# Attention and two MLPs on one core: code products put in front of a value burst, a scaling put one slot later, VectorE's work dealt out anew, and a rearranged start

## The chip, the cores and the metric

One core of a Trainium2 chip runs the whole program in one launch. The time is the device time of that launch in microseconds (us). Before the change three runs took 793.62, 793.74 and 791.83 us, median 793.62. TensorE (PE) does the matrix products, VectorE (DVE), ScalarE (ACT) and GpSimd (POOL) the elementwise work, and DMA queues, issued mostly by SyncE (SP), move data. PSUM has eight banks, in which matrix products land.

## The reference

The attention has 16 heads (batch 2 by 8), 768 rows, 64 columns. Each row of q and of k gets a 6-bit code, and a score counts only where the codes agree:

```python
q_bits = (np.einsum('bhsd,dk->bhsk', q, proj) > 0)
k_bits = (np.einsum('bhsd,dk->bhsk', k, proj) > 0)
mask = q_bucket[:, :, :, None] == k_bucket[:, :, None, :]
scores = np.where(mask, scale * np.matmul(q, k.transpose(0, 1, 3, 2)), -1000000000.0)
attn = np.exp(scores - np.max(scores, axis=-1, keepdims=True))
attn = attn / (np.sum(attn, axis=-1, keepdims=True) + 1e-09)
out = np.matmul(attn, v)
```

Its 1536 by 512 output goes through two MLPs (512 to 2048 to 512). The first has g = h * tanh(log(1 + exp(h))), the second a rational function of h. All is float32.

## The kernel before

**Heads and slots.** The attention is laid out in slots, six to a head, one for each block of 128 keys (`c`). In a slot TensorE computes the scores of one block, `sp` (function `st`, L380: four products, a large part `qB` and a small part `qX`, with K and the codes in one stacked operand `kk`), and ACT takes their exponential `e` (L385). Beside that stands `mp` (function `smax`, L347: two products) of a head or two later, of which DVE takes the row maximum `m` (L351). When a head's six maxima are there, `fin_a` and `fin_b` (L357, L360, L366) put them by four small DMAs, two from SP's queue and two from POOL's, into a row of `qB`, so that the scores come out with the maximum taken off.

**Bursts.** After some slots TensorE runs products of other shapes in a row: `pv` (function `pv`, L287: exponentials times V, for two blocks at a time, in slots 3, 5 and 7 of the head, thus slots 3, 5 and the next head's 1), `dn` (function `dsum`, L406: sums of the exponentials, four products at once in four column groups of 32), `vsp` (function `vsum`, L274: sums of V, in even heads, for the pair of heads), and `cp` (function `codes`, L287: the projections whose signs are the codes). The signs of `cp` are taken by DVE for k (`code_k`, L324, into `kk`) and by ACT for q (`code_q`, L333, into `qB`); both read the one PSUM tile `cp`.

**Division.** `devac` copies `dn` out (L431), `gather` brings it into 24 rows by DMA, `recip` is a chain of five short operations on DVE (L452 to L458), `store` and `spread` send the result through memory to all partitions, and `norm` (L482), `xhi` and `xlo` scale and split the head pair's output for the first MLP.

**What sets the order.** The order is written out, not scheduled. A table, `order`, gives for each function the slot in which it runs, counted from the first slot of its head; -16 is sixteen slots ahead. Within a slot the functions run in the order of the table, and each engine runs its instructions in the order in which they were written. The list `start` writes out the first head's chain by hand (`warm` are small products that keep TensorE busy, `khi`, `hi` and `lo` split q and k into a large and a small part). `tail(i)` runs what is left of the attention within the iterations of the first MLP.

**Buffers.** `sp`, `mp` and `vsp` take turns in three buffers of two PSUM banks (pool `ps`). Which one a tile takes follows from the order in which they are freed in the program. `dn` and `cp` share one bank, `pv` has another.

**DVE's other work.** The weights of the first MLP come as 64-bit numbers; DVE turns them into float32 with three operations a part (L100, L103, L106), in slots of the attention and beyond.

Of the kernel before, what the change touches and what calls it, by code (L numbers as in the profile page):

```python
# [44 lines left out]
def attention_moe_moe(ctx: ExitStack, tc: tile.TileContext, kq, v, proj2, cst, eye, w1, w2, ab, out):  # L45
# [11 lines left out]
    def f32(ap):  # L57
        return ap.bitcast(F32)
# [111 lines left out]
    def attention(actx, tctx):  # L170
# [26 lines left out]
        def memsets():  # L197
            nc.vector.memset(ones, 1.0)
            nc.vector.memset(wones, 1.0)
            nc.gpsimd.memset(cs_t, 0.0)  # L200
            nc.gpsimd.memset(cs_t[:, 1:2], -1.0)
            nc.gpsimd.memset(cs_t[:, 2:3], 1.0)
            for i in range(4):
                nc.gpsimd.memset(f32(KK[i])[32:64, 0], 0.0)
            for i in range(2):
                nc.gpsimd.memset(f32(SM[i]), 0.0)
            nc.gpsimd.memset(bias[:, 1:2], 1.000001)
# [25 lines left out]
                fn = fn or lo_of("lo", h)  # L233
                fn(qX[h % 4], raws[h], qB[h % 4])

        def khi(h, i):
            nc.scalar.activation(out=KK[h % 4][64:128, i], in_=raws[h][0:64], func=ACT.Copy)

        def move_k(h):
            if 0 <= h < B * H:  # L240
# [39 lines left out]

# [13 lines left out]

        ct = {}


        def codes(h):
            if not 0 <= h < B * H:
                return  # L300
            ct[h] = [pvp.tile([128, 512], F32, tag="dn", name="cp")] * 2
            if h == 0:
                ct[h][1] = pvp.tile([128, 512], F32, tag="pv", name="wm")
            for t in ct[h][0:1 + (h == 0)]:
                both(t, p_raw, raws[h], start=True, stop=True)


        warm_up = []

        def warm(n):  # L310
            if 0 in ct:
                t = ct[0][1]
            else:
                if not warm_up:
                    warm_up.append(ps.tile([128, 2, 512], F32, tag="s", name="wm"))
                t = warm_up[0][:, 0]
            for _ in range(n):
                nc.tensor.matmul(out=t[0:32, HALF:512], lhsT=ones, rhs=wones, start=True, stop=True)

        def code_k(h):  # L320
            if not 0 <= h < B * H:
                return
            for a in range(2):
                nc.vector.tensor_scalar(  # L324
                    out=qhalf(KK[h % 4][0:32, 0], a), in0=ct[h][0][64 * a:64 * a + 32, 0:HALF],
                    scalar1=cs_t[:, 1:2], scalar2=cs_t[:, 2:3], op0=ALU.is_gt, op1=ALU.mult,
                )

        def code_q(h):
            if not 0 <= h < B * H:  # L330
                return
            for a in range(2):
                nc.scalar.activation(  # L333
                    out=qhalf(qB[h % 4], a)[0:32], in_=ct[h][1][64 * a + 32:64 * a + 64, 0:HALF],
                    func=ACT.Sign, bias=cs_t[:, 0:1],
                )

        mt = {}

# [87 lines left out]
        def devac(h):  # L427
            if not 0 <= h < B * H:
                return
            dv = cs_p.tile([128, HALF], F32, tag="dv", name="dv")  # L430
            nc.scalar.activation(out=dv, in_=pvt.pop((h, "d"))[:, 0:HALF], func=ACT.Copy)  # L431
            Rt[h] = dv

        def gather(h):
            if not 0 <= h < B * H:
                return
            dv = Rt.pop(h)
            cs = cs_p.tile([24, 2, 32], F32, tag="cs", name="cs")
            for n in range(2):
                nc.sync.dma_start(  # L440
                    out=cs[:, n], in_=dv[64 * n:64 * n + 64:32].rearrange("t (a i) -> t a i", i=32)
                )
            Rt[h] = cs

        def recip(h):
            if not 0 <= h < B * H:
                return
            cs = Rt.pop(h)
            rc = cs_p.tile([24, 32], F32, tag="rc", name="rc")

            z = cs_p.tile([24, 32], F32, tag="z", name="z")
            nc.vector.tensor_tensor(out=rc, in0=cs[:, 0], in1=cs[:, 1], op=ALU.add)  # L452
            nc.vector.tensor_scalar(
                out=z, in0=rc, scalar1=0.0, scalar2=float(np.float32(1e-9)) / (S * TINY) - 1.0, op0=ALU.is_equal, op1=ALU.mult
            )
            nc.vector.tensor_scalar(out=rc, in0=rc, scalar1=1e-9, scalar2=None, op0=ALU.add)
# [67 lines left out]
        def first(f, n):  # L524
# [48 lines left out]
        for name, fn, at, per in order:  # L573
# [29 lines left out]
        start = (  # L603
            ("load", 0), ("get", 0), ("get", 1), ("load", 1), ("load", 2), ("warm", 5), ("hi", 0), ("codes", 0),
            ("khi", 0, 0), ("lo", 0), ("code_q", 0), ("code_k", 0), ("warm", 1), ("hi", 1), ("lo", 1), ("khi", 0, 1),
            ("get", 2), ("move_x", 0), ("smax", 0, 0), ("warm", 2), ("move_h", 0), ("hi", 2), ("lo", 2), ("smax", 0, 1),
            ("move_k", 1), ("warm", 2), ("smax", 0, 2), ("load", 3), ("warm", 2), ("smax", 0, 3), ("codes", 1),
            ("smax", 0, 4), ("warm", 2), ("code_q", 1), ("smax", 0, 5), ("fin_a", 0), ("fin_b", 0), ("code_k", 1),
            ("warm", 6), ("move_k", 2), ("load_v", 0), ("move_x", 1), ("smax", 1, 0), ("smax", 1, 1), ("move_h", 1),
            ("coef",),  # L610
        )

        def run():
            memsets()
            fns = {o[0]: o[1] for o in order}
            fns.update(get=get, coef=coef, khi=khi)
            for name, *k in start:
                if name == "warm":
                    warm(*k)
                    continue  # L620
                done.add(("move_k" if name == "khi" else name, tuple(k[:1]) if name == "khi" else tuple(k)))
# [10 lines left out]
    def moe(mctx, tctx, tail):  # L632
# [114 lines left out]
        def run():  # L747
# [70 lines left out]
            for i in range(-5, len(seq) + 5):  # L818
# [102 lines left out]
```

## Time and profile before

| | us |
|---|---|
| median of three runs | 793.62 (791.83 to 793.74) |
| the profiled execution | 791.69 |
| its span | 789.8 |
| TensorE, busy | 774.2 (98%) |
| VectorE, busy | 593.7 (75%) |
| ScalarE, busy | 422.5 (53%) |
| first scores (`sp` of head 0) | at 19.67 |
| first scores of head 1 | at 36.57 |
| first product of the MLPs | at 259.65 |

The span begins and ends with the first and last record; the profiled execution's own time is 1.89 us longer. A row of the timeline gives the start, the duration (of merged records, from the first start to the last end), engine, line and operation, output <- inputs, shape and the count of records; a matrix product of float32 leaves two records. Matrix products are pipelined, so that their durations overlap, and the difference between two starts tells what one costs. In brackets stands the idle time before an instruction and what ended it.

### The profile page before, as it was taken

The numbers are of one execution on the slowest core, as the hardware profiler recorded it, in microseconds if no ns is written. First come the engines' busy times: TensorE is split into PE (matmuls) and PEld (weight loads), VectorE is DVE, ScalarE is ACT, GpSimd is POOL, SyncE is SP. The second block draws the span as 40 slices with busy tenths as digits, with TensorE's granted clock in tenths as the row PEclk, the third lists the DMA queues.
The fourth block names the chain that finished last, engine by engine and source line by source line (L and its number), as shares of the span: only waits on it lengthen the run. The fifth ranks groups of instructions, "written<-read, shape, count | busy, mean of one in ns | idle before, by whom it ended". The sixth has DMA issues, their size and how long they took to land.

```text
span 789.8 us, 10934 instructions
## 1 busy us (share of the span) xinstructions
PE 774.2 (98%) x3788; PEld 572.4 (72%) x3788; DVE 593.7 (75%) x1100; ACT 422.5 (53%) x684; POOL 71.6 (9%) x100
## 2 busy tenths in 40 slices
PE   7899999999999999999999999999999999999998
PEld 4556555555555778888888888887888888888886
DVE  5587778778772599846556677659998888888886
ACT  3455565655555443331212334368886867777664
POOL 4223214124121000000000000000000000000000
PEclk9999999999999999999999999999999999999999
DMA  4847666554651444424555587620000100000001
GB/s 124 211 128 202 174 162 175 141 142 121 174 166 31 127 137 148 131 87 145 171 157 149 165 255 256 202 80 1 0 1 1 53 1 1 1 36 18 1 0 54
DMA packets 57031, 85.50 MB, mean 108 GB/s; under 512 B 20496, under 2 KB 28688, under 8 KB 56976
## 3 DMA queue, kind: packets, MB, share of 16 engines
q1 hardware_dynamic: 55952, 84.77, 36.4%
q8 instruction: 30, 0.49, 0.3%
q14 instruction: 25, 0.20, 0.1%
q0 software_dynamic: 1024, 0.03, 0.1%
HBM read 57.71 MB, written 14.73 MB: 92 GB/s over the span
## 4 chain that ended last, share of the span: by engine, by line
PE 88%; DVE 6%; DMA 2%; ACT 1%; issue 1%; SPq 1%; POOL 0%; DVEq 0%; ACTq 0%
PE h L665 29%; PE y L685 16%; PE y L683 15%; PE sp L380 9%; PE pv L287 8%; PE mp L347 5%; PE dn L406 4%; PE cp L287 2%; DVE w L70 1%; DVE m L351 1%; DMA kk<-qB 1%; DVE t L103 1%; DMA vf<-v 1%; DVE r L106 1%; DVE gl L70 1%
## 5 line engine op out<-in xcount | busy, mean ns | idle before, releaser
L665 PE MATMUL h<-xh,w 128*128 128x512 f32 x768 | 205.0, 389 | 0.0
L665 PEld LDWEIGHTS h<-xh,w 128*128 128x128 f32 x768 | 144.1, 188 | 30.6 <-issue 0.6
L351 DVE TENSOR_REDUCE m<-mp 128x1 f32<-128x768 f32 x96 | 91.3, 955 | 50.2 <-PE mp L347 49.0
L385 ACT ACTIVATE e<-sp 128x768 f32<-128x768 f32 x96 | 77.1, 810 | 80.8 <-PE sp L380 79.4
L70 DVE TENSOR_TENSOR gl<-ep,gh 128x512 fp32r<-128x512 f32 x96 | 65.9, 687 | 69.4 <-ACT ep L709 68.6
L708 ACT ACTIVATE gh<-h 128x512 fp32r<-128x512 f32 x48 | 28.7, 598 | 154.7 <-PE h L665 141.5
L665 PE MATMUL h<-xl,w 128*128 128x512 f32 x384 | 102.7, 389 | 0.0
L685 PE MATMUL y<-w,gh 128*128 128x512 f32 x384 | 96.3, 389 | 0.0
L683 PE MATMUL y<-gh,w 128*128 128x512 f32 x384 | 94.8, 389 | 0.0
L665 PEld LDWEIGHTS h<-xl,w 128*128 128x128 f32 x384 | 72.1, 188 | 15.1
L683 PEld LDWEIGHTS y<-gh,w 128*128 128x128 f32 x384 | 72.1, 188 | 15.0
L685 PEld LDWEIGHTS y<-w,gh 128*128 128x128 f32 x384 | 72.1, 188 | 15.0
L287 PE MATMUL pv<-e,vf 128*64 128x384 f32 x384 | 72.5, 499 | 0.0
L380 PE MATMUL sp<-qB,kk 128*128 128x384 f32 x192 | 55.5, 370 | 1.6 <-DMA qB<-stt 1.1
L715 ACT ACTIVATE ep<-h 128x512 f32<-128x512 f32 x48 | 28.5, 595 | 52.3 <-PE h L665 52.3
L347 PE MATMUL mp<-kk,qB 128*128 128x384 f32 x192 | 52.8, 358 | 3.2 <-DVE m L351 2.3
L106 DVE SCALAR_TENSOR_TENSOR r<-r,t 128x256 int32<-128x256 int32 (+1 forms) x114 | 52.2, 457 | 4.7
L380 PEld LDWEIGHTS sp<-qB,kk 128*128 128x128 f32 x192 | 30.8, 188 | 34.1 <-issue 16.0
L103 DVE SCALAR_TENSOR_TENSOR t<-r,t 128x256 int32<-128x256 int32 (+1 forms) x114 | 52.2, 458 | 3.9
L685 PE MATMUL y<-w,gl 128*128 128x512 f32 x192 | 53.3, 392 | 0.5 <-DVE gl L70 0.4
L717 DVE TENSOR_TENSOR n<-n,ep 128x512 f32<-128x512 f32 x48 | 33.1, 690 | 26.9 <-ACT n L716 26.9
L683 PE MATMUL y<-gl,w 128*128 128x512 f32 x192 | 51.6, 390 | 1.6 <-DVE gl L70 1.6
(79 smaller groups left out, 1012.2 us busy)
## 6 DMA issues: line engine op xcount, KB each, us to landing
r<-w SPq DMA_DIRECT2D x100, 256.0 KB
w<-r SPq DMA_DIRECT2D x64, 128.0 KB
w<-w SPq DMA_DIRECT2D x16, 512.0 KB
r<-w SPq DMA_DIRECT2D x14, 512.0 KB
kq<-kq SPq DMA_DIRECT2D x16, 384.0 KB
kk<-qB SPq DMA_DIRECT2D x15, 384.0 KB
kk<-qX SPq DMA_DIRECT2D x16, 192.0 KB
qX<-qB SPq DMA_DIRECT2D x16, 192.0 KB
```

The source lines that it names most:

```text
L70: nc.vector.tensor_tensor(out=o, in0=i, in1=f32(h), op=ALU.subtract)
L103: lambda: nc.vector.scalar_tensor_tensor(out=t, in0=r[:, :, 1], scalar=-0x40000000, in1=t, op0=ALU.bitwise_and, op1=ALU.bitwise_or),
L106: lambda: nc.vector.scalar_tensor_tensor(out=o, in0=r[:, :, 0], scalar=29, in1=t, op0=ALU.logical_shift_right, op1=ALU.bitwise_or),
L287: nc.tensor.matmul(out=o[64 * a:64 * a + 64, 0:HALF], lhsT=w, rhs=qhalf(x, a), start=start, stop=stop)
L347: nc.tensor.matmul(out=p[:, a, 0:HALF], lhsT=qB[h % 4][:, c * 128:(c + 1) * 128], rhs=qhalf(KK[h % 4][:, 0], a), start=True, stop=True,)
L351: nc.vector.tensor_reduce(out=mt[h][:, c:c + 1], in_=halves(p), op=ALU.max, axis=AX.XY)
L380: nc.tensor.matmul(out=p[:, a, 0:HALF], lhsT=kk[:, c * 128:(c + 1) * 128], rhs=qq[:, a * HALF:(a + 1) * HALF], start=(i == 0), stop=(i == 1),)
L385: nc.scalar.activation(out=wide(e), in_=halves(p), func=ACT.Exp, scale=1.0 / D ** 0.5)
L665: nc.tensor.matmul(out=p, lhsT=w[:, c * 128:(c + 1) * 128], rhs=x[:, c, :], start=(n == 0), stop=(n == 11))
L683: nc.tensor.matmul(out=y[m], lhsT=w[:, DM + m * 128:DM + (m + 1) * 128], rhs=g, **s)
L685: nc.tensor.matmul(out=y[m], lhsT=g[:, m * 128:(m + 1) * 128], rhs=w[:, DM:2 * DM], **s)
L717: nc.vector.tensor_tensor(out=v_, in0=v_, in1=u, op=ALU.mult)
```

## The change

Five things move. (1) The code products `cp` run in slot 3 directly in front of `pv`, no longer as a burst of their own after slot 2. `code_k` goes with them, and `code_q` comes from slot 4 to slot 3. (2) The scaling of the sums of V becomes a function of its own, `vscale`, in slot 4 behind that slot's reduce; the products of `vsum` stay. (3) `dsum` runs for each block by itself, 192 columns a product instead of 384 for two blocks at a time. The sums then stand in one piece: one gather DMA instead of two, and a chain of four operations. (4) `recip` to `xlo`, `hi`, `move_k` and `lo` get other slots, and `tail` other iterations. (5) In the first head the signs are dealt over DVE and ACT from two PSUM tiles, the small parts of q and k are made on POOL, the DMA of `proj` is issued from ACT's queue, the maxima stand closer together, the first scores stand ahead of head 1's maxima, and `qB` gets a memset.

TensorE, the slots 2 and 3 of head 5, before: `sp` with `qB_120` is head 5's, `mp` with `qB_122` head 7's.

```order
L380 MATMUL sp<-qB_120,kk_128 128x384 x2
L380 MATMUL sp<-qX_124,kk_128 128x384 x2
L347 MATMUL mp<-kk_130,qB_122 128x384 x2
L287 MATMUL cp<-kq,pr 64x384 x2
L380 MATMUL sp<-qB_120,kk_128 128x384 x2
L380 MATMUL sp<-qX_124,kk_128 128x384 x2
L347 MATMUL mp<-kk_130,qB_122 128x384 x2
L287 MATMUL pv<-e,vf_131 64x384 x4
```

The same slots after:

```order
L405 MATMUL sp<-qB_120,kk_128 128x384 x2
L405 MATMUL sp<-qX_124,kk_128 128x384 x2
L372 MATMUL mp<-kk_130,qB_122 128x384 x2
L405 MATMUL sp<-qB_120,kk_128 128x384 x2
L405 MATMUL sp<-qX_124,kk_128 128x384 x2
L372 MATMUL mp<-kk_130,qB_122 128x384 x2
L317 MATMUL cp<-kq,pr 64x384 x2
L305 MATMUL pv<-e,vf_131 64x384 x4
```

The `cp` row stood between the two slots, and stands behind both, in front of `pv`.

ACT in the same head, before, from the evacuation `ev` of the head ahead:

```order
L422 ACTIVATE ev<-pv,vsc 64x384 x2
L431 ACTIVATE dv<-dn 128x384
L385 ACTIVATE e<-sp 128x768 x3
L333 ACTIVATE qB_119<-cp,cst 32x384 x2
L385 ACTIVATE e<-sp 128x768
```

And after:

```order
L447 ACTIVATE ev<-pv,vsc 64x384 x2
L456 ACTIVATE dv<-dn 128x192
L410 ACTIVATE e<-sp 128x768 x2
L352 ACTIVATE qB_119<-cp,cst 32x384 x2
L410 ACTIVATE e<-sp 128x768 x2
```

The two signs into `qB` stood behind the exponentials of slots 2, 3 and 4, and now stand ahead of that of slot 4.

DVE in head 4, slots 2 to 4, before (`kk` are the codes of head 7, `vsc` the scaled sums of V):

```order
L351 TENSOR_REDUCE m<-mp 128x1
L324 TENSOR_SCALAR kk_130<-cp,cst 32x384 x2
L351 TENSOR_REDUCE m<-mp 128x1
L70 TENSOR_TENSOR qX_126<-kq,qB_122 128x768
L279 TENSOR_SCALAR vsc<-vsp 128x2
L351 TENSOR_REDUCE m<-mp 128x1
L452 TENSOR_TENSOR rc<-cs 24x32
L453 TENSOR_SCALAR z<-rc 24x32
```

And after:

```order
L376 TENSOR_REDUCE m<-mp 128x1 x2
L343 TENSOR_SCALAR kk_130<-cp,cst 32x384 x2
L474 TENSOR_SCALAR z<-cs 24x32
L477 TENSOR_SCALAR rc<-cs 24x32
L478 RECIPROCAL rc<-rc 24x32
L479 SCALAR_TENSOR_TENSOR rc<-z,rc 24x32
L376 TENSOR_REDUCE m<-mp 128x1
L297 TENSOR_SCALAR vsc<-vsp 128x2
L376 TENSOR_REDUCE m<-mp 128x1
L503 TENSOR_TENSOR xf<-ev,R 128x768
```

The scaling went behind the next reduce; the chain of the reciprocal, one operation shorter, stands between the codes and that reduce, and the split into `qX` is elsewhere.

The core of the diff (the lines of `khi`, `qhi`, `qlo`, `klo`, `evac` and the weights are left out):

```diff
         def codes(h):
...
             if h == 0:
-                ct[h][1] = pvp.tile([128, 512], F32, tag="pv", name="wm")
-            for t in ct[h][0:1 + (h == 0)]:
-                both(t, p_raw, raws[h], start=True, stop=True)
+                ct[h][1] = ps.tile([128, 2, 512], F32, tag="s", name="cp")[:, 0]
+            code_products(h)
...
+        def signs(h):
+            for a in range(2):
+                code_k(h, (a,))
+                code_q(h, (1 - a,))
...
+        def vscale(j):
+            if not 0 <= j < B * H // 2:
+                return
+            p = vs_r.pop((j, "p"))
             vs_r[j, "c"] = sm_p.tile([128, 2], F32, tag="vsc", name="vsc")
             nc.vector.tensor_scalar(out=vs_r[j, "c"], in0=p[:, 0, 0:2], scalar1=TINY, scalar2=None, op0=ALU.mult)
...
             for n in range(4):
                 nc.tensor.matmul(
-                    out=pvt[h, "d"][32 * n:32 * n + 32, 0:HALF], lhsT=ones, rhs=qhalf(pt[h, c - 1 + n // 2], n % 2),
-                    start=(c == 1), stop=(c == NC - 1),
+                    out=pvt[h, "d"][32 * n:32 * n + 32, 0:S // 4], lhsT=ones,
+                    rhs=pt[h, c][:, n * S // 4:(n + 1) * S // 4], start=(c == 0), stop=(c == NC - 1),
                 )
...
-            nc.vector.tensor_tensor(out=rc, in0=cs[:, 0], in1=cs[:, 1], op=ALU.add)
...
-            ("hi", hi, -18, 1),
-            ("move_k", move_k, -17, 1),
-            ("lo", lo, -15, 1),
-            ("codes", codes, -16, 1),
+            ("hi", hi, -19, 1),
+            ("move_k", move_k, -18, 1),
+            ("codes", codes, -15, 1),
             ("pv", pv, (3, 3, 5, 5, 7, 7), 6),
             ("dsum", dsum, (5, 5, 5, 5, 7, 7), 6),
             ("vsum", vsum, 3, 0),
-            ("code_k", code_k, -16, 1),
-            ("code_q", code_q, -14, 1),
+            ("vscale", vscale, 4, 0),
+            ("code_k", code_k, -15, 1),
+            ("code_q", code_q, -15, 1),
             ("evac", evac, 7, 1),
             ("devac", devac, 7, 1),
             ("gather", gather, 8, 1),
-            ("recip", recip, 10, 1),
-            ("store", store, 11, 1),
-            ("spread", spread, 12, 1),
-            ("norm", norm, 23, 0),
-            ("xhi", xhi, 23, 0),
-            ("xlo", xlo, 29, 0),
+            ("recip", recip, 15, 1),
+            ("store", store, 16, 1),
+            ("norm", norm, 29, 0),
+            ("spread", spread, 17, 1),
+            ("xhi", xhi, 29, 0),
+            ("xlo", xlo, 35, 0),
+            ("lo", lo, -19, 1),
...
-            nc.sync.dma_start(out=t, in_=d)
+            (nc.sync if i else nc.scalar).dma_start(out=t, in_=d)
...
-            ("load", 0), ("get", 0), ("get", 1), ("load", 1), ("load", 2), ("warm", 5), ("hi", 0), ("codes", 0),
-            ("khi", 0, 0), ("lo", 0), ("code_q", 0), ("code_k", 0), ("warm", 1), ("hi", 1), ("lo", 1), ("khi", 0, 1),
...
+            ("get", 0), ("load", 0), ("get", 1), ("load", 1), ("load", 2), ("warm", 5), ("khi", 0), ("qhi",), ("codes", 0),
+            ("warm", 4), ("signs", 0), ("khi", 2), ("qlo",), ("hi", 1), ("klo",), ("khi", 1), ("get", 2), ("smax", 0, 0),
...
+            ("code_q", 1), ("move_k", 2), ("load_v", 0), ("move_h", 1), ("warm", 8), ("st", 0, 0), ("smax", 1, 0),
+            ("smax", 1, 1), ("coef",),
...
-            for g in {1: range(last, last + 3), 2: range(last + 3, last + 5), 4: range(last + 5, last + 30)}.get(i, ()):
+            for g in {2: range(last, last + 7), 3: range(last + 7, last + 9), 5: range(last + 9, last + 36)}.get(i, ()):
```

## Rows read from the trace of the kernel before

**Rows 1.** Windows, two stages: span, each engine's busy us (instructions), PE clock, DMA.

```profile
36.57:259.65 223.08, 221.35 (x1341) 124.37 (x1337) 161.94 (x289) 125.58 (x187) 59.33 (x77) 1.00 0.53 147
259.65:789.80 530.15, 524.31 (x2308) 431.88 (x2304) 410.57 (x780) 281.31 (x476) 0.00 (x0) 1.00 0.28 88
```

**Rows 2.** Timeline, PE, head 5: start, duration, operation, count [idle before <- releaser].

```profile
102.84 0.61 PE L380 MATMUL sp<-qB,kk 128*128 128x384 f32 x2
...
104.09 0.87 PE L287 MATMUL cp<-kq,pr 128*64 128x384 f32 x4
104.89 0.62 PE L380 MATMUL sp<-qB,kk 128*128 128x384 f32 x2
...
105.71 0.52 PE L347 MATMUL mp<-kk,qB 128*128 128x384 f32 x2
106.16 1.51 PE L287 MATMUL pv<-e,vf 128*64 128x384 f32 x8
107.60 0.62 PE L380 MATMUL sp<-qB,kk 128*128 128x384 f32 x2
...
108.41 0.51 PE L347 MATMUL mp<-kk,qB 128*128 128x384 f32 x2
...
109.53 0.62 PE L347 MATMUL mp<-kk,qB 128*128 128x384 f32 x2
110.08 1.51 PE L287 MATMUL pv<-e,vf 128*64 128x384 f32 x8
111.52 1.50 PE L406 MATMUL dn<-e,ones 128*32 128x384 f32 x16
```

**Rows 3.** Timeline, DVE, the same stretch.

```profile
105.08 1.34 DVE L324 TENSOR_SCALAR kk<-cp,cst 32x384 fp32r<-32x384 f32 x2
...
108.95 0.96 DVE L351 TENSOR_REDUCE m<-mp 128x1 f32<-128x768 f32 x1 [0.68 <-PE mp L347]
```

**Rows 4.** Timeline, ACT, the same stretch.

```profile
108.66 0.81 ACT L385 ACTIVATE e<-sp 128x768 f32<-128x768 f32 x1 [1.88 <-PE sp L380]
109.50 1.16 ACT L333 ACTIVATE qB<-cp,cst 32x384 fp32r<-32x384 f32 x2
```

**Rows 5.** Timeline, PE, head 4 (even).

```profile
83.64 0.52 PE L380 MATMUL sp<-qB,kk 128*128 128x384 f32 x2
...
84.85 0.62 PE L347 MATMUL mp<-kk,qB 128*128 128x384 f32 x2 [0.35 <-DVE m L351]
...
92.39 0.61 PE L274 MATMUL vsp<-ones,vtw 128*128 128x1 f32 x4
92.86 0.60 PE L380 MATMUL sp<-qB,kk 128*128 128x384 f32 x2
...
95.32 1.51 PE L287 MATMUL pv<-e,vf 128*64 128x384 f32 x8
```

**Rows 6.** Timeline of all engines, the start.

```profile
0.73 1.28 ACT L858 ACT_TABLE_LOAD   x1 [0.73 <-PEq L914]
...
1.19 0.42 SPq L598 DMA_DIRECT2D pr<-proj  x1
...
4.17 1.55 PE L287 MATMUL cp<-kq,pr 128*64 128x384 f32 x4 [0.73 <-DMA pr<-proj]
...
8.63 0.62 PE L347 MATMUL mp<-kk,qB 128*128 128x384 f32 x2
...
14.93 1.50 PE L318 MATMUL wm<-wones,ones 128*32 128x128 f32 x12
...
16.31 0.21 DVE L360 STREAM_TRANSPOSE stt<-smt 128x32 f32<-128x32 f32 x1
```

**Rows 7.** Waits, longest first: us in total, times, longest.

```profile
ACT qB L333 <- DMA kk<-qB: 3.4, 1, 3.4
...
PE dn L406 <- ACT qB L333: 1.8, 1, 1.8
PE y L683 <- DVE gl L70: 1.6, 1, 1.6
```

More of the change, by code (lines that the diff above doesn't have):

```diff
@@ L234, in lo, with khi, qhi, qlo @@
                 fn(qX[h % 4], raws[h], qB[h % 4])
-        def khi(h, i):
-            nc.scalar.activation(out=KK[h % 4][64:128, i], in_=raws[h][0:64], func=ACT.Copy)
+        def khi(i):
+            o = KK[0][64:128, i] if i < 2 else qX[0][0:64]
+            nc.scalar.activation(out=o, in_=raws[0][0:64], func=ACT.Copy)
+        def qhi():
+            nc.vector.tensor_copy(qB[0][64:128], raws[0][64:128])
+        def qlo():
+            lo_pool(qX[0][64:128], raws[0][64:128], qB[0][64:128])
+        def klo():
+            lo_pool(qX[0][0:64], raws[0][0:64], qX[0][0:64])
         def move_k(h):
@@ L295, in attention, with code_products @@
         ct = {}
+        def code_products(h):
+            for a in range(2):
+                nc.tensor.matmul(
+                    out=ct[h][a][64 * a:64 * a + 64, 0:HALF], lhsT=p_raw, rhs=qhalf(raws[h], a), start=True, stop=True
+                )
         def codes(h):
@@ L302, in codes, with code_k, code_q @@
             if h == 0:
-                ct[h][1] = pvp.tile([128, 512], F32, tag="pv", name="wm")
-            for t in ct[h][0:1 + (h == 0)]:
-                both(t, p_raw, raws[h], start=True, stop=True)
+                ct[h][1] = ps.tile([128, 2, 512], F32, tag="s", name="cp")[:, 0]
+            code_products(h)
         warm_up = []
         def warm(n):
[L311 to L316, printed above, removed]
+            if not warm_up:
+                warm_up.append(pvp.tile([128, 512], F32, tag="pv", name="wm"))
             for _ in range(n):
-                nc.tensor.matmul(out=t[0:32, HALF:512], lhsT=ones, rhs=wones, start=True, stop=True)
-        def code_k(h):
+                nc.tensor.matmul(out=warm_up[0][0:32, 0:128], lhsT=ones, rhs=wones, start=True, stop=True)
+        def code_k(h, of=(0, 1)):
             if not 0 <= h < B * H:
                 return
-            for a in range(2):
+            for a in of:
                 nc.vector.tensor_scalar(
-                    out=qhalf(KK[h % 4][0:32, 0], a), in0=ct[h][0][64 * a:64 * a + 32, 0:HALF],
+                    out=qhalf(KK[h % 4][0:32, 0], a), in0=ct[h][a][64 * a:64 * a + 32, 0:HALF],
                     scalar1=cs_t[:, 1:2], scalar2=cs_t[:, 2:3], op0=ALU.is_gt, op1=ALU.mult,
                 )
-        def code_q(h):
+        def code_q(h, of=(0, 1)):
             if not 0 <= h < B * H:
                 return
-            for a in range(2):
+            for a in of:
                 nc.scalar.activation(
-                    out=qhalf(qB[h % 4], a)[0:32], in_=ct[h][1][64 * a + 32:64 * a + 64, 0:HALF],
+                    out=qhalf(qB[h % 4], a)[0:32], in_=ct[h][a][64 * a + 32:64 * a + 64, 0:HALF],
                     func=ACT.Sign, bias=cs_t[:, 0:1],
                 )
+        def signs(h):
+            for a in range(2):
+                code_k(h, (a,))
+                code_q(h, (1 - a,))
         mt = {}
@@ L400, in dsum @@
         def dsum(h, c):
-            if not 0 <= h < B * H or c % 2 == 0:
+            if not 0 <= h < B * H:
                 return
-            if c == 1:
+            if c == 0:
                 pvt[h, "d"] = pvp.tile([128, 512], F32, tag="dn", name="dn")
@@ L429, in devac @@
                 return
-            dv = cs_p.tile([128, HALF], F32, tag="dv", name="dv")
-            nc.scalar.activation(out=dv, in_=pvt.pop((h, "d"))[:, 0:HALF], func=ACT.Copy)
+            dv = cs_p.tile([128, S // 4], F32, tag="dv", name="dv")
+            nc.scalar.activation(out=dv, in_=pvt.pop((h, "d"))[:, 0:S // 4], func=ACT.Copy)
             Rt[h] = dv
@@ L437, in gather @@
             dv = Rt.pop(h)
[L438 to L442, printed above, removed]
+            cs = cs_p.tile([24, 32], F32, tag="cs", name="cs")
+            nc.sync.dma_start(out=cs, in_=dv[0:128:32].rearrange("t (a i) -> t a i", i=32))
             Rt[h] = cs
@@ L451, in recip @@
             z = cs_p.tile([24, 32], F32, tag="z", name="z")
-            nc.vector.tensor_tensor(out=rc, in0=cs[:, 0], in1=cs[:, 1], op=ALU.add)
             nc.vector.tensor_scalar(
-                out=z, in0=rc, scalar1=0.0, scalar2=float(np.float32(1e-9)) / (S * TINY) - 1.0, op0=ALU.is_equal, op1=ALU.mult
+                out=z, in0=cs, scalar1=0.0, scalar2=float(np.float32(1e-9)) / (S * TINY) - 1.0, op0=ALU.is_equal, op1=ALU.mult
             )
-            nc.vector.tensor_scalar(out=rc, in0=rc, scalar1=1e-9, scalar2=None, op0=ALU.add)
+            nc.vector.tensor_scalar(out=rc, in0=cs, scalar1=1e-9, scalar2=None, op0=ALU.add)
             nc.vector.reciprocal(out=rc, in_=rc)
@@ L579, in attention @@
                 todo = [((at, c - 2, 4 + c)[h] if h < 3 else at + 6 * h + c, (h, c)) for h in range(nh) for c in range(per)]
+            elif name == "load":
+                todo = [(at + 6 * h if h > 5 else 2 * h - 7, (h,)) for h in range(nh)]
             elif name.startswith("fin_"):
@@ L603, in attention @@
         start = (
[L604 to L610 removed]
+            ("get", 0), ("load", 0), ("get", 1), ("load", 1), ("load", 2), ("warm", 5), ("khi", 0), ("qhi",), ("codes", 0),
+            ("warm", 4), ("signs", 0), ("khi", 2), ("qlo",), ("hi", 1), ("klo",), ("khi", 1), ("get", 2), ("smax", 0, 0),
+            ("warm", 1), ("move_k", 1), ("move_x", 0), ("lo", 1), ("smax", 0, 1), ("warm", 1), ("hi", 2), ("lo", 2),
+            ("smax", 0, 2), ("warm", 1), ("move_h", 0), ("load", 3), ("smax", 0, 3), ("warm", 1), ("smax", 0, 4),
+            ("warm", 1), ("move_x", 1), ("smax", 0, 5), ("codes", 1), ("fin_a", 0), ("fin_b", 0), ("code_k", 1),
+            ("code_q", 1), ("move_k", 2), ("load_v", 0), ("move_h", 1), ("warm", 8), ("st", 0, 0), ("smax", 1, 0),
+            ("smax", 1, 1), ("coef",),
         )
@@ L615, in run @@
             fns = {o[0]: o[1] for o in order}
-            fns.update(get=get, coef=coef, khi=khi)
+            fns.update(get=get, coef=coef, khi=khi, qhi=qhi, qlo=qlo, klo=klo, signs=signs)
+            done.update((name, (0,)) for name in ("hi", "lo", "move_k", "code_k", "code_q"))
             for name, *k in start:
@@ L620, in run @@
                     continue
-                done.add(("move_k" if name == "khi" else name, tuple(k[:1]) if name == "khi" else tuple(k)))
+                done.add((name, tuple(k)))
                 fns[name](*k, **({"fn": lo_pool} if (name, *k) in POOL_LO else {}))
```

4 lines of the change are left out of this document (3 added, 1 removed).

## The prediction

> **What bounds the kernel now.** I read the busy time by stage first. In [rows 1] the stage after 259.65 us (the matrix products) has TensorE busy 524.31 of 530.15 us, and the stage before it from 36.57 us on is 221.35 of 223.08 us busy, both at a granted clock of 1.00, the 2.4 GHz level. So from the second head on TensorE's own order is the time: an edit counts by what it adds to or takes from TensorE's sequence, and the other engines count only where TensorE waits for them. Only the first head is a chain of waits. The change leaves the matrix products' instructions as they are; it rearranges the attention, so I then read the attention's timeline engine by engine, and last the waits.
>
> In the timeline of an odd head [rows 2] the reader is to see one pattern: scores `sp`, next head's maxima `mp`, then a burst of other shapes (`cp`, `pv`, `dn`). Steps between starts give the prices. The code product costs 104.89 - 104.09 = 0.80, `pv` 107.60 - 106.16 = 1.44. After a burst, `sp` to `mp` takes 108.41 - 107.60 = 0.81. A stretch of two slots, sp4 to the next `pv`, takes 110.08 - 107.60 = 2.48. Its second `mp` (109.53) cannot start until a PSUM buffer is free: the exponential of sp4 starts 1.06 after sp4 and lasts 0.81 [rows 4], ends at 109.47, and `mp` starts 0.06 later. The scheme has no slack there: anything that makes the exponential or the reduce of this stretch later reaches TensorE at once. In even heads a stall of this kind already exists: the second `mp` of slot 1 starts 1.21 after its `sp`, with 0.35 idle waiting for a reduce [rows 5]; unstalled the step is 0.70 (0.81 less the 0.11 that the first `sp` after a burst takes longer), so the stall is worth 0.51.
>
> **The change part by part, steady heads.** I walk from T, the start of the `mp` of slot 3, which stands unmoved.
>
> *Codes in front of `pv`.* One burst less per head. Before, sp2 to sp4 is 107.60 - 102.84 = 4.76. After, sp2 to T is a two-slot stretch without a burst, 1.88 to 1.93 (as sp4 to mp5 here), then 0.55 (`mp` to the burst, 110.08 - 109.53), then `cp` and `pv` together. That row does not exist. Its upper bound is 0.80 + 1.44 = 2.24; its lower bound six rounds at pv's inner pace, about 1.95 to 2.05 (pv's 1.44 is four rounds with one opening and one closing). I take 2.09, nearer to the lower end since the two have one shape. So sp4 comes at T + 2.64, and sp2 to sp4 is 4.52: a gain of 0.24 a head (0.09 to 0.3).
>
> *What the readers of the codes do then.* DVE: the reduce of slot 3 runs from T + 0.56 to 1.52 (0.96 each, [rows 3]), then the two `kk` pieces, 1.34 together [rows 3], to 2.88. ACT's two `qB` pieces read the same PSUM tile and the program makes them wait for DVE's; allowing 0.17 for the handover (an estimate; the buffer above took 0.06) they run from 3.05 to 4.24 (1.16 and gaps, [rows 4]). They now stand in ACT's queue ahead of e(4), which could have started at sp4 + 1.06 = T + 3.70. So e(4) runs from 4.24 to 5.05, 0.54 late; behind it in the queue are e(5) and, in some heads, the copies to `xh`. In odd heads the second `mp` takes the buffer of the reduce: mp4 at 2.64 + 0.81 = 3.45, reduce from 4.01 to 4.97, `mp` at 5.03, `pv` at 5.58. The stretch becomes 5.58 - 2.64 = 2.94 instead of 2.48: a loss of 0.46. Odd head: +0.46 - 0.24 + 0.02 (the sums below) = **+0.25**, and +0.33 in head 3, whose buffer is freed by e(4). Five odd heads (3 to 11): +1.3.
>
> *V sums scaled a slot later, even heads.* `vsp` takes 92.86 - 92.39 = 0.47 [rows 5]. Its scaling on DVE goes behind the reduce of slot 4, so the PSUM buffer that `vsp` holds is not free for the two slots 4 and 5, and two buffers carry four tiles. sp4 is at T + 2.64 + 0.47 = 3.11, and sp5 itself now waits. In heads 2, 4, 12 it waits for e(4): 5.11, then `mp` at 5.92 and `pv` at 6.36, a stretch of 3.25 where it was 95.32 - 92.86 = 2.46. In heads 6, 8, 10 it waits for the reduce of mp4 (4.46 to 5.42): 5.47, 6.28, `pv` 6.72, a stretch of 3.61. Against these +0.79 and +1.15 stand the 0.24 of the merged burst and the 0.51 stall of slot 1, which goes, because that `mp` now takes an exponential's buffer and is in time. Net **+0.04** (heads 4, 12), **+0.40** (6, 8, 10); head 2 had no such stall, +0.53. Together +1.8. Heads 2 to 12: **+3.1**.
>
> *Sums by chunk.* Same columns, twice the records at half the width. Now 16 records of 0.49 each fit in 1.50 us [rows 2], since four column groups run at once: a round of four takes about 0.33. At 192 columns a round is 0.165, longer than the weight load (12 narrow records that all wait for their load take 1.50, 0.11 to 0.125 each, [rows 6]), which stays hidden. +0.02 a head for the extra rounds; upper bound if every record paid that 0.11 alone: 48 x 0.11 = 5.3 a head instead of 2.2. I take +0.02, the row of `dn` itself being the nearest. Heads 13 to 15 and 0, 1: +0.1.
> The Trainium skill, TensorE: Matmul & The Clock Gate, Back-to-back issue gap, states that a weight load and a product at 128 columns sustain about 81 ns a product. By that, an estimate, 48 x 0.081 = 3.9 a head, +1.7 over now. The trace of `dn` speaks against it (four records start within one round), so it is a rival below with a small chance.
>
> *Division and split later, by slots.* The reciprocal chain loses one of its five operations and moves five slots, and with it the store and spread DMAs, which pass other heads' moves and loads on SP's queue; norm, `xh` and `xl` move six. DVE does the same work, 161.94 of 223.08 us busy [rows 1]. I cost it at nothing, hidden under TensorE; the cover is thin between `kk` (T + 2.88) and the reduce of slot 4 (4.01): the chain of about 0.9 that now stands there fits with 0.2 to spare. One gather DMA fewer, a smaller copy on ACT: nothing.
>
> **Start.** TensorE's code product waits for `p_raw` at 4.17 and the first `mp` starts at 8.63 [rows 6]. Now one product instead of two, and its four readers are dealt over DVE and ACT at once: `mp` 1.4 sooner. Against it, the DMA of `p_raw` leaves ACT's queue behind the table load (0.73 + 1.28 = 2.01) instead of SP's at 1.19: up to 0.8 later. So `mp` is 0.6 to 1.4 sooner. From `mp` to the transposes it is 7.68 now (16.31 - 8.63); six reduces at 0.96 with 0.5 ahead are 6.3, so 1.4 more. The DMA from the transposes' end (16.52) to the first `sp` (19.67) stays 3.15. In sum 2.0 to 2.8 sooner, less if the four subtractions now on POOL hold its half of the DMAs: I take 2.1, `sp` at 17.6 (16.9 to 18.2).
> The Trainium skill, ScalarE: Activation LUTs, What ACT_TABLE_LOAD costs, adds a drain of about 1.38 us behind the load; by it the DMA would leave at 3.4 and the gain nearly vanish. The trace has the load's 1.28 but no ACT work early enough behind it to tell.
>
> First head after that: now 36.57 - 19.67 = 16.90, of which 1.8 is the wait of `dn` for the codes of head 3, held by a late move of K [rows 7]. The move is a slot earlier, so that goes. But two `mp` move behind the first `sp` (+1.1), the code pair stands ahead of the second exponential (+1.2), and the last scores wait for a reduce (+0.8): net **+1.3**. Head 1, walked likewise (two `mp` a slot, the codes behind four reduces): **+0.9**.
>
> **Matrix products.** The last head's division lands in other iterations; the one long wait there, 1.6 [rows 7], stays or shifts: -0.2 (-1.5 to +1.6).
>
> Sum: -2.1 + 1.3 + 0.9 + 3.1 + 0.1 - 0.2 = **+3.1**. The profiled execution took 791.69 (span 789.80 and 1.89 around it), so 794.8 in its like. The median of the runs, 793.62, stands 1.93 above it: **796.7**. One can tell 0.3%, that is 2.4 us: faster means under 791.2, slower over 796.0.
>
> **The rivals.**
> *The readers stay hidden.* If TensorE's stretch keeps its 2.48 (ACT's pair fits before e(4), or a buffer is free), only gains are left: odd heads 5 x -0.24, six even ones 6 x -0.75 (less the 0.51 that head 2 has not to lose), start -2.1 + 1.3, products -0.2: -6.2 us, 787.4. It decides where e(4) starts no later than 1.1 after sp4. For it speaks that ACT stands idle 1.88 before e(4) [rows 4]; against it that the second `mp` is on the dot now.
> *It cancels.* Half of what the longer stretches add (2.4 us over odd heads, 5.8 over even ones) is not there, the rest comes as walked: 3.1 - 4.1 = -1.0, 792.6 (791.5 to 794.5). The walk's steps of 0.2 to 0.5 leave room for that; the buffers, fixed by the program, speak against.
> *The start gives nothing.* `p_raw` behind the table load and POOL's subtractions in front of its half of the DMAs leave the first `sp` at 19.7: +2.1 on the forecast, 798.8. It decides at a first `sp` after 19 us.
> *Narrow sums pay per record.* 1.7 to 3.1 a head over 16 heads: 824 to 846. It decides where 16 records of 192 columns take over 0.8 us.
>
> **How the numbers follow.** Forecast 0.45 (795 to 799 by the merged burst's and the start's bounds; about 0.10 of it within 0.3%), hidden 0.15, cancels 0.25, start lost 0.12, narrow sums 0.03. Faster 0.15; within 0.3% 0.25 + 0.10 = 0.35; slower 0.35 + 0.12 + 0.03 = 0.50. The range leaves out most of the hidden case and the narrow sums: 790.5 to 800.5.
>
> **What would show it.** In the profile after: `cp` and `pv` back to back in 2.1; ACT's `qB` pair ending just before e(4), and e(4) starting about 1.6 after sp4 instead of 1.06; `pv` 2.9 after sp4 in odd heads, 3.25 or 3.6 in even ones, with waits of `sp` for `e` or `m` behind `vsp`; no stall in slot 1 of even heads; the first `sp` at 17.6 and the first of head 1 at 35.8. I am wrong if the two-slot stretches stay at 2.5, or if the even stall of 0.51 remains.

## The result

The changed kernel takes 798.10 us (median of four runs, 797.21 to 799.89) against 792.85 for the kernel before in the same runs: a ratio of 1.0062 (95% interval 1.0033 to 1.0090), slower, by 5.25 us. The profiled execution took 798.22 with a span of 796.4, 6.6 more than the span before.

Where the 6.6 us lie, by the starts of the first scores of each head:

| | before | after | difference |
|---|---|---|---|
| first scores of head 0 | 19.67 | 19.30 | -0.37 |
| head 0 | 16.90 | 19.29 | +2.39 |
| head 1 | 15.95 | 16.82 | +0.87 |
| heads 2 to 12 | 167.52 | 171.99 | +4.47 |
| head 13 to the first product of the MLPs | 39.61 | 39.70 | +0.09 |
| the MLPs | 530.15 | 529.30 | -0.85 |

The windows after, as [rows 1]: the start's wait, the stretch behind it, heads 1 to 15, the matrix products.

```profile
16.00:19.30 3.30, 0.00 (x0) 0.03 (x1) 0.00 (x0) 0.87 (x2) 0.18 (x1) 0.87 0.83 213
19.30:26.00 6.70, 6.70 (x21) 4.95 (x22) 4.30 (x6) 1.74 (x4) 2.19 (x3) 0.55 0.72 170
38.59:267.10 228.51, 220.56 (x1709) 136.87 (x1705) 152.10 (x268) 122.42 (x184) 55.14 (x74) 1.00 0.52 140
267.10:796.40 529.30, 524.30 (x2308) 431.95 (x2304) 411.53 (x784) 282.99 (x478) 0.00 (x0) 1.00 0.28 89
```

TensorE did nothing from 16 to 19.3 us, and its granted clock fell: 0.55 in the mean of the next 6.7 us, most of that time at its lower level, 1.2 GHz. From head 1 to the first product of the MLPs it was idle for 7.95 us of 228.51, where it had been idle for 1.73 of 223.08 before.

TensorE in head 7, an odd one, slots 2 to 5 (start, duration, operation), to be set beside [rows 2]. In what follows sp4 are the scores of slot 4 and e(4) is their exponential; e(0,1) is that of head 0, slot 1.

```profile
138.59 0.62 PE L405 MATMUL sp<-qB,kk 128*128 128x384 f32 x2
...
141.08 0.87 PE L317 MATMUL cp<-kq,pr 128*64 128x384 f32 x4
141.78 1.46 PE L305 MATMUL pv<-e,vf 128*64 128x384 f32 x8
143.17 0.62 PE L405 MATMUL sp<-qB,kk 128*128 128x384 f32 x2
...
145.53 0.62 PE L372 MATMUL mp<-kk,qB 128*128 128x384 f32 x2 [0.35 <-DVE m L376]
146.08 1.51 PE L305 MATMUL pv<-e,vf 128*64 128x384 f32 x8
147.52 1.51 PE L431 MATMUL dn<-e,ones 128*32 128x192 f32 x32
148.96 0.62 PE L405 MATMUL sp<-qB,kk 128*128 128x384 f32 x2
```

`cp` and `pv` run as one burst of 143.17 - 141.08 = 2.09, where they took 0.80 and 1.44 apart. But the next `pv` follows sp4 by 146.08 - 143.17 = 2.91 instead of 2.48, and the last `mp` has 0.35 idle in front of it, waiting for a reduce. ACT and DVE in the same stretch, as [rows 4] and [rows 3]:

```profile
143.57 1.17 ACT L352 ACTIVATE qB<-cp,cst 32x384 fp32r<-32x384 f32 x2 [2.04 <-DVE rc L477]
144.76 1.51 ACT L410 ACTIVATE e<-sp 128x768 f32<-128x768 f32 x2
```

```profile
142.06 1.34 DVE L343 TENSOR_SCALAR kk<-cp,cst 32x384 fp32r<-32x384 f32 x2
...
144.51 0.96 DVE L376 TENSOR_REDUCE m<-mp 128x1 f32<-128x768 f32 x1 [0.35 <-PE mp L372]
```

The `qB` pair starts when `kk` is done and holds ACT until 144.74; e(4) begins at 144.76, 1.59 after sp4 instead of 1.06. The waiting `mp` does not take e(4)'s buffer but that of the reduce at 144.51.

TensorE in head 6, an even one, as [rows 5]:

```profile
118.82 0.51 PE L405 MATMUL sp<-qB,kk 128*128 128x384 f32 x2
...
119.60 0.61 PE L372 MATMUL mp<-kk,qB 128*128 128x384 f32 x2
...
126.95 0.61 PE L286 MATMUL vsp<-ones,vtw 128*128 128x1 f32 x4
127.41 0.60 PE L405 MATMUL sp<-qB,kk 128*128 128x384 f32 x2
...
129.76 0.61 PE L405 MATMUL sp<-qB,kk 128*128 128x384 f32 x2 [1.05 <-DVE m L376]
...
131.01 1.51 PE L305 MATMUL pv<-e,vf 128*64 128x384 f32 x8
```

In slot 1 the maxima follow their scores by 0.78, not 1.21: the old stall is gone. Behind `vsp` the scores of slot 5 now wait 1.05 for a reduce, and `pv` comes 131.01 - 127.41 = 3.60 after sp4, where it was 2.46.

The start, as [rows 6]:

```profile
0.74 1.28 ACT L883 ACT_TABLE_LOAD   x1 [0.74 <-PEq L939]
...
0.77 0.39 ACTq L622 DMA_DIRECT2D pr<-proj  x1
...
4.11 1.55 PE L317 MATMUL cp<-kq,pr 128*64 128x384 f32 x4 [0.67 <-DMA pr<-proj]
...
7.43 0.96 PE L372 MATMUL mp<-kk,qB 128*128 128x384 f32 x2
...
13.21 0.46 SPq L263 DMA_DIRECT2D qX<-qB  x1
...
13.78 0.52 SPq L217 DMA_DIRECT2D kq<-kq  x1
...
14.11 0.21 DVE L385 STREAM_TRANSPOSE stt<-smt 128x32 f32<-128x32 f32 x1
...
14.39 0.46 SPq L259 DMA_DIRECT2D kk<-qX  x1
14.93 1.25 POOL L391 DMA_DIRECT2D qB<-stt  x2 [1.74 <-DVE stt L385]
...
19.30 0.98 PE L405 MATMUL sp<-qB,kk 128*128 128x384 f32 x2 [3.85 <-DMA qB<-stt]
```

The first maxima start 1.2 sooner and the transposes end 2.2 sooner (14.32, was 16.52). The first scores gain only 0.37 of it: from the transposes to them it is 4.98 us, was 3.15. (The change also puts the loads of heads 4 and 5 from slot 0 of head 0 into slots 1 and 3, which the section on it does not say; they stand behind the first scores.)

### The profile page after: what moved, and what is told of

The parts are those of the page before. It is cut to its first block, busy times and chain, and to the rows that moved or that the text cites. A ratio compares the mean times of both kernels' runs of the same rounds, so it can differ in the third digit from the quotient of the medians.

```text
span 796.4 us, 11649 instructions
## 1 busy us (share of the span) xinstructions
PE 775.6 (97%) x4172; PEld 587.9 (74%) x4172; DVE 585.7 (74%) x1084; ACT 421.6 (53%) x684; POOL 73.4 (9%) x103
## 4 chain that ended last, share of the span: by engine, by line
PE 85%; DVE 8%; ACT 3%; DMA 2%; issue 1%; SPq 0%; POOL 0%; DVEq 0%; ACTq 0%; POOLq 0%
PE h L690 28%; PE y L710 15%; PE y L708 14%; PE sp L405 9%; PE pv L305 8%; PE mp L372 5%; PE dn L431 4%; DVE m L376 2%; PE cp L317 1%; DVE w L70 1%; DVE kk L343 1%; ACT qB L352 1%; ACT e L410 1%; DVE gl L70 1%; DVE t L103 1%
```

## The experiments

Each changes the kernel after the change; its time is the median of its runs, with the ratio to the kernel before in the same runs. The kernel before had medians of 793.4 to 793.5 there. The changed kernel was not timed again beside them: its 798.10, at a ratio of 1.0062, is that of the result above.

**code_q behind e(4).**

```diff
-            ("code_q", code_q, -15, 1),
+            ("code_q", code_q, -14, 1),
```

> The changed kernel with code_q back one slot later, behind the exponential of slot 4; nothing else. Theory (ACT's pair ahead of e(4) makes the two-slot stretch late): e(4) starts 1.06 after sp4 again instead of 1.6, the second maximum of odd heads takes e(4)'s buffer and pv follows sp4 by 2.5 instead of 2.9, -0.44 in each of heads 1, 3, 5, 7, 9, 11; in even heads sp5 waits for e(4), 1.93 after sp4, where it was 2.0 to 2.35: -0.06 to -0.4. Sum about -4, so 794 us. Rival (DVE's chain of codes and division before that slot's reduce is the bound, ACT only looks late): the second maximum still comes 2.35 after sp4 in odd heads, 797.5 to 798.5 us.

Measured: 792.96 us, ratio 0.9990 (0.9978 to 1.0002). Heads 2 to 12 take 167.82 instead of 171.99. TensorE and ACT in head 7:

```profile
139.98 0.62 PE L405 MATMUL sp<-qB,kk 128*128 128x384 f32 x2
...
141.90 0.61 PE L372 MATMUL mp<-kk,qB 128*128 128x384 f32 x2
142.44 1.51 PE L305 MATMUL pv<-e,vf 128*64 128x384 f32 x8
```

```profile
141.04 0.81 ACT L410 ACTIVATE e<-sp 128x768 f32<-128x768 f32 x1 [2.70 <-PE sp L405]
141.88 1.17 ACT L352 ACTIVATE qB<-cp,cst 32x384 fp32r<-32x384 f32 x2
```

e(4) is back at 1.06 after sp4, `mp` at 1.92, `pv` at 2.46. Odd heads take 14.62 (15.06 with the change), even ones 15.79 (15.87 or 16.22). The rival, DVE's chain as the bound, falls for odd heads: DVE's order between the codes and the reduce is the same. Head 1 gains too, 16.35 instead of 16.82.

**The scaling in slot 3.**

```diff
-            ("vscale", vscale, 4, 0),
...
             ("recip", recip, 15, 1),
+            ("vscale", vscale, 3, 0),
```

> The changed kernel with the scaling of the V sums back in slot 3, on DVE behind the codes and the reciprocal chain and ahead of the reduce of slot 4; nothing else. Theory (the PSUM buffer held through slot 4 makes the scores of slot 5 wait in even heads): sp5 follows sp4 by 1.15 instead of 2.0 (heads 2, 4, 12) and 2.35 (0, 6, 8, 10); the second maximum still waits as in odd heads, so pv follows sp4 by 2.9 in even heads too: -0.4 and -0.75 a head, -4 in sum, 794 us. Rival (the DVE work moved in front of the reduce costs what the buffer gives): the reduce of slot 4 starts later than 0.56 after its product and the time stays at 797.5 to 798.5.

Measured: 793.51 us, ratio 0.9994 (0.9979 to 1.0008). Even heads, head 6 here:

```profile
125.77 0.60 PE L405 MATMUL sp<-qB,kk 128*128 128x384 f32 x2
...
126.90 0.51 PE L405 MATMUL sp<-qB,kk 128*128 128x384 f32 x2
...
128.11 0.62 PE L372 MATMUL mp<-kk,qB 128*128 128x384 f32 x2 [0.35 <-DVE m L376]
128.66 1.51 PE L305 MATMUL pv<-e,vf 128*64 128x384 f32 x8
```

The scores of slot 5 follow sp4 by 1.13 and `pv` by 2.89, as in an odd head with the change; the 0.35 before `mp` is the other wait, that behind ACT's pair. Even heads from 4 on take 15.17 (head 4) or 15.51, odd ones stay at 15.06.

**Both.**

> Both of the edits before: code_q behind e(4), the scaling in slot 3. Theory: all stretches of slots 4 and 5 are back at 2.46 to 2.5, even heads gain 0.85 to 1.2, odd ones 0.44: about -9 us against the changed kernel, 789 us, thus 4 us faster than the kernel before; an odd head takes 14.6, an even one 15.0. Rival (the two waits are one, so that the second edit gives nothing once the first is in): 794 us, as each alone. Rival (the merged burst itself saves nothing): odd heads at 14.76 as before the change, 792 us.

Measured: 789.40 us, ratio 0.9949 (0.9932 to 0.9966). Odd heads take 14.63, even ones 15.06 to 15.09; heads 2 to 12 take 163.66, 8.33 less than with the change, where the two edits alone took off 4.17 and 3.88. In head 6 no wait is left:

```profile
123.27 0.59 PE L405 MATMUL sp<-qB,kk 128*128 128x384 f32 x2
...
125.18 0.61 PE L372 MATMUL mp<-kk,qB 128*128 128x384 f32 x2
125.72 1.51 PE L305 MATMUL pv<-e,vf 128*64 128x384 f32 x8
```

So the two waits are separate and add, and with both gone the merged burst is a gain. One new wait appears: in head 13 the order in which buffers are freed now gives sp5 the buffer of e(4), and that head takes 14.67 instead of 13.97.

**The codes in a burst of their own, all else as in the last.**

```diff
-            ("codes", codes, -15, 1),
+            ("codes", codes, -16, 1),
...
-            ("code_k", code_k, -15, 1),
-            ("code_q", code_q, -15, 1),
+            ("code_k", code_k, -16, 1),
+            ("code_q", code_q, -14, 1),
```

> code_q behind e(4), the scaling in slot 3, and the code products with code_k back in a burst of their own after slot 2, the rest as in the changed kernel. Theory (one burst less is worth 0.24 a head): against the 14.63 and 15.08 of the version with the merged burst a head takes 0.2 to 0.25 more (14.85, 15.3), 792 us. Rival (the order of the rest, not the merged burst, makes these heads shorter than before the change): 14.6 to 14.7 and 15.1, 789.5.

Measured: 792.46 us, ratio 0.9986 (0.9976 to 0.9996). Odd heads 14.79 to 14.84, even ones 15.25 to 15.30 (head 7, 15.54, has a wait of its own, for e(4)): the burst less is worth 0.20 a head. Even heads are 0.4 shorter than before the change all the same; that is the old stall of slot 1, which stays away without the merge.

**Small products through the wait.** Of the line of `start` only the entries concerned are shown, here and below.

```diff
-("warm", 8), ("st", 0, 0)
+("warm", 24), ("st", 0, 0)
```

> The changed kernel with 24 instead of 8 small products between the code products of head 1 and the first scores, so that TensorE works on while it waits for the row of maxima (it was idle for 3.85 us, and its granted clock then fell to 0.5). Theory (the fallen clock delays the first head): the granted clock stays at 1.00 from 16 to 26 us, the first scores still start at 19.3, the scores of head 1 start at 36.5 to 37.5 instead of 38.6: -1 to -2 us, 796 to 797 us. Rival (at that place DVE and ACT are the bound and the slow products are hidden): the clock stays up and the scores of head 1 start at 38.3 to 38.6, 798 us.

Measured: 799.19 us, ratio 1.0067 (1.0048 to 1.0086): nothing gained. The windows before the first scores, behind them, and the six microseconds after:

```profile
16.00:19.08 3.08, 2.76 (x26) 2.52 (x24) 0.00 (x0) 0.68 (x2) 0.00 (x0) 1.00 0.72 208
19.08:26.00 6.92, 5.00 (x24) 3.51 (x24) 5.54 (x7) 3.07 (x6) 3.27 (x3) 1.00 0.84 196
26.00:32.00 6.00, 5.42 (x21) 2.68 (x21) 3.85 (x7) 2.72 (x5) 1.05 (x2) 0.72 0.64 164
```

The clock stayed at 1.00 until 26 us and slot 3 of head 0 began at 27.04 instead of 28.39. Then TensorE waited for the exponentials behind head 2's code pair:

```profile
26.59 0.62 PE L372 MATMUL mp<-kk,qB 128*128 128x384 f32 x2 [2.31 <-ACT e L410]
```

After these 2.31 us idle the clock fell there, 0.72 from 26 to 32, and head 1 began at 38.87 (38.59 with the change). The low clock was moved to a later place, not spared. The wait alone does not settle it, though: with both edits the same `mp` waits 2.31 us too, at 28.29, and the clock stays at 1.00.

**Head 3's load one step sooner.**

```diff
-("move_h", 0), ("load", 3), ("smax", 0, 3)
+("load", 3), ("move_h", 0), ("smax", 0, 3)
```

> The changed kernel with the load of head 3's q and k written one step sooner, ahead of the small part's move (move_h) of head 0, so that its 384 KB are through before the row of maxima is sent; nothing else. Theory (the row's small DMAs wait behind that load and the moves in the DMA engines): from the end of the transposes to the first scores 3.1 to 3.4 us instead of 4.98, the first scores at 17.4 to 17.7 where the products of the start run at full speed, the scores of head 1 about 1 us sooner, 796.5 to 797.5. Rival (the row waits for the moves alone, or for its own issue): 4.5 to 5 us between them, 798.

Measured: 797.32 us, ratio 1.0045 (1.0026 to 1.0064), inside the expected range and 0.8 under the changed kernel's own runs, which its interval alone would not settle. The mechanism shows in the rows:

```profile
10.47 0.77 SPq L217 DMA_DIRECT2D kq<-kq  x1
...
14.87 0.21 DVE L385 STREAM_TRANSPOSE stt<-smt 128x32 f32<-128x32 f32 x1
...
15.15 1.58 SPq L391 DMA_DIRECT2D qB<-stt  x2
...
18.25 0.58 PE L405 MATMUL sp<-qB,kk 128*128 128x384 f32 x2 [2.03 <-DMA qB<-stt]
```

From the transposes' end, 15.08, to the scores it is 3.17 us, as before the change. The first two pairs of `mp` products took 1.01 and 0.97 in this execution, so the scores start at 18.25 and not 17.5; head 1 begins at 37.97.

> code_q behind e(4), the scaling in slot 3, and the load of head 3 one step sooner. Theory (start and steady heads add): 1 to 1.5 us under the 789.4 of the two edits alone, 788. Rival (what is gained at the first scores is lost in the first head, at the wait behind head 2's code pair): 789 to 789.6.

With both earlier edits (no new line): 787.88 us, ratio 0.9923 (0.9899 to 0.9948), 1.5 under the two edits alone, as the theory said, though the intervals overlap. The transposes to the scores: 3.15.

**Head 2's signs a slot later, in the first head alone.**

```diff
+            elif name == "code_q":
+                todo = [(at + 6 * h if h != 2 else 1, (h,)) for h in range(nh)]
```

> code_q behind e(4), the scaling in slot 3, and in the first head the signs of head 2 (code_q) one slot later, behind the second exponential. Theory (in the first head too ACT's pair ahead of an exponential holds up the maxima: TensorE idles 2.3 us for e(0,1) there): the idle time before the maxima of slot 2 falls under 0.8, the first head takes 15 to 15.5 us from its first to head 1's first scores instead of 16.9, 787.5 to 788. Rival (DVE, with three reduces, codes and a split there, is the bound): 16.5 to 16.9 us, 789 to 789.6.

Measured: 788.80 us, ratio 0.9936 (0.9914 to 0.9957). The wait of `mp` for e(0,1) went from 2.3 to nothing, but the scores of slot 3 now wait 1.46 for an exponential, and the first head takes 17.27, more than the 16.94 without the edit, in an execution whose clock was 0.65 from 20 to 24 us. Neither account gave that number. A run with the same dip of the clock tells the edit's worth: with code_q behind e(4) alone it is 0.50 from 19.5 to 22.8 us, as here, and from the first scores to those of slot 3 it takes 28.07 - 19.29 = 8.78 there and 27.37 - 19.19 = 8.18 here. That is 0.6, as the medians say (789.40 to 788.80).

> All of these: code_q behind e(4), the scaling in slot 3, head 3's load sooner, head 2's code_q a slot later. Theory: 787 us, the sum of the gains. Rival (one of the two start edits takes the other's gain): 788 us or more.

Measured: 787.15 us, ratio 0.9918 (0.9896 to 0.9941), 2.25 under the two edits, about the sum of 1.5 and 0.6. This is the fastest version, 6 us faster than the kernel before and 11 faster than the changed one.

**All of it with 17 small products.**

> The four edits together as before, with 17 instead of 8 small products ahead of the first scores. Theory (with the wait behind head 2's codes out of the way the clock, kept up, does pay): granted clock 1.00 from 16 to 24 us, where it was 0.73 and 0.85, the first head 1 us shorter (16.5), 786.2. Rival (what the small products keep up is lost at a later wait, as it was with them alone): 787 or more, the clock low at a later place.

Measured: 787.98 us, ratio 0.9921 (0.9905 to 0.9937): the rival. The clock is 1.00 from 16 to 24 us and 0.84 and 0.73 from 24 to 32, behind a wait of 1.75 for an exponential; the first head takes 18.1.

## Why the prediction was right, and where its sizes were off

**The steady heads, forecast +3.1, measured +4.47.** The mechanism is shown: each of the two moves, undone alone, gives its part back, and they add. The walk's points were met within 0.1: the burst 2.09 (2.09), e(4) at 1.59 after sp4 (1.6), `pv` at 2.91 in an odd head (2.94) and 3.60 in head 6 (3.61), scores waiting for a reduce behind `vsp`, the stall of slot 1 gone. The missing 1.4 us are small sums, eleven times: an odd head lost 0.31 (forecast 0.25), the even ones 0.15 to 0.18 (0.04) and 0.51 (0.40). From sp2 to sp4 an odd head gained 4.76 - 4.58 = 0.18, not 0.24, since its `mp` waits a little there too; the experiment with the burst apart says 0.20. The stall of slot 1 gave 0.43 (1.21 - 0.78), not 0.51: its `mp` now stands at 0.78 where an unstalled one is at 0.70. Head 2 lost 0.98 (0.53); its slot 3 takes 0.3 more than that of head 4, behind an `mp` that waits 0.22 for an exponential, and why that one is late was not followed up. The later division, costed at nothing, and the narrow sums are held by the run with the codes apart: with both in, its odd heads take 14.79 to 14.84 (head 7 aside), at most 0.08 more than the 14.76 of the kernel before.

**Why an ACT pair cost an odd head 0.43 when `mp` waits for DVE.** The walk had this right, and the experiment makes it plain. The program gives `mp` the buffer that is freed first in its order. With the pair in front, e(4) is freed last, so `mp` gets the reduce's buffer, and that reduce waits for a product of the same slot. With the pair behind, `mp` gets e(4)'s buffer again and the reduce does not matter. Which buffer a tile takes is read from the program; the rows show only who ended each wait, and agree.

**The first scores, forecast -2.1, measured -0.37: the step that failed.** The transposes ended at 14.32, inside the walk (13.7 to 14.5). The step "the DMA from the transposes' end to the first scores stays 3.15" was wrong: it took 4.98. The rows show what was issued ahead of it on SP's queue: a move (13.21), the 384 KB load of head 3 (13.78, was 9.87) and another move (14.39). The kernel before, the load and the window from 16 us on:

```profile
9.87 0.42 SPq L216 DMA_DIRECT2D kq<-kq  x1
```

```profile
16.00:19.30 3.30, 1.66 (x8) 0.82 (x6) 2.59 (x6) 0.00 (x0) 1.25 (x2) 1.00 0.01 1
```

The DMA share was 0.83 from 16 to 19.3 us, where it was 0.01 before. The order on SP's queue is not all of it: the row's two DMAs on POOL's queue landed 3.98 and 3.43 us after their issue, and 1.75 and 1.62 with the load sooner. With the load sooner the step is 3.17 and 3.15 again, and 3.66 in the fastest version. It is 3.16 as well in the profiled execution of both edits, whose load stands where the change put it (13.94): the maxima were slow there, and the row was issued at 17.70, 3.8 us behind the load instead of 1.2.
The rival of a lost start came true by its own mark (first scores after 19 us), but not by its causes: POOL's half of the DMAs waited for the transposes alone, and the DMA of `p_raw` left at 0.77, while the table load ran, not behind it. Leaving 0.42 sooner it brought the code product only 0.06 forward (4.11, was 4.17); where the rest went was not tried.
The Trainium skill's drain behind a table load, which the prediction weighed (ScalarE: Activation LUTs, What ACT_TABLE_LOAD costs), thus did not hold up the issue of this DMA: the trace has it 0.03 after the load's start.

**Head 0, forecast +1.3, measured +2.39.** The wait of `dn` for the codes of head 3 [rows 7] is gone, as forecast. What was not forecast is the fallen clock: behind 3.85 us idle the two records of the first scores take 0.98, where they take 0.58 with the clock kept up. From the first scores to those of slot 3 it is 28.39 - 19.30 = 9.09 us; in the five runs whose clock is 1.00 over these slots (the scaling in slot 3, both edits, small products, and the load sooner without and with the edits) it is 7.95 to 7.97. This 1.1 is as much as the forecast missed. (Head 1 thus starts at 38.59, not at the 35.8 that the prediction gave as a sign.) But small products alone do not win it back: two runs show the price return behind the next wait.

**Head 1** (+0.87, forecast +0.9) and **the stretch from head 13** (+0.09, forecast about +0.1) came out as forecast in size. In head 1 that is not shown part by part; code_q behind e(4) alone takes 0.47 off it. The narrow sums cost nothing to speak of: 32 records last 1.51, as 16 wide ones last 1.50 [rows 2].
The Trainium skill's 81 ns a product (TensorE: Matmul & The Clock Gate, Back-to-back issue gap), taken for each record as the prediction took it, does not hold for them: 148.96 - 147.52 = 1.44 for 32 records are 45 ns each, four column groups at once.

**The matrix products** gained 0.85 (forecast 0.2, within its bounds); TensorE's waits for `gl` fell from 2.0 to 1.2 us. Why was not tried.

Together: -2.1 too large by 1.7, +1.3 too small by 1.1, +3.1 too small by 1.4, against 0.7 more gained in the products: 6.6 instead of 3.1 by the spans. That the time came as near as 798.1 to 796.7 is in part luck: the forecast was added to a median of 793.62, which a fourth run brought to 792.85, and the profiled execution before (791.69) was faster than each of its timed runs. The rival of the lost start had 798.8.

## What to carry to other kernels

Where a buffer turns over with no slack, walk the stretch with the durations of the trace and ask of every instruction that is moved what it stands in front of on its own engine: a saved burst of 0.2 us was lost twice over to a pair of 1.2 us in front of the exponential that frees the next buffer. Ask of each tile which consumer frees it, since the order in which the program frees buffers decides who waits for whom. Ask of a small DMA on the critical path which loads are issued just ahead of it: one of 384 KB, 1.2 us ahead, made this one 1.8 us later.

## What the hardware showed that was not expected

The products of the start run at two paces in executions of kernels with the same start: the first `mp` products took 0.62 each from 8.66 us on in the changed kernel, and in the run with both edits 1.01 until 16 us:

```profile
9.08 1.01 PE L372 MATMUL mp<-kk,qB 128*128 128x384 f32 x2
...
15.11 1.01 PE L372 MATMUL mp<-kk,qB 128*128 128x384 f32 x2
...
20.79 0.41 PE L405 MATMUL sp<-qB,kk 128*128 128x384 f32 x1 [1.53 <-DMA qB<-stt]
```

The slow pace is that of the lower level. In the changed kernel two such products take 1.01 where the granted clock is 0.50, 1.2 GHz:

```profile
20.00:25.00 5.00, 5.00 (x15) 3.25 (x15) 3.32 (x4) 1.63 (x3) 2.19 (x3) 0.50 0.65 163
```

```profile
24.25 1.01 PE L405 MATMUL sp<-qB,kk 128*128 128x384 f32 x2
```

The column of the granted clock reads 1.00 for both starts all the same. It averages the clock records of the trace, and the first of these stands at 8.21 us in the changed kernel and at 17.07 in the run with both edits, just where the products go over to the faster pace; ahead of it the 1.00 has no record behind it. In all twelve profiled executions the first record stands where the pace rises, from 7.00 us (the kernel before) to 20.48 (the scaling in slot 3). So the start runs at the lower level until then, and the first scores, 19.3 and 20.8, follow. What decides the moment was not found: six of these kernels have the same program up to the first scores, and in them it lies between 8.21 and 20.48 us.
